# One weight load of a decode kernel, issued as four loads of unequal partition counts

## The chip, the core and the metric

The kernel runs on one core of one Trainium2 chip. A core has a matrix engine (TensorE, PE), a vector engine (VectorE, DVE), an activation engine (ScalarE, ACT), a general engine (GpSimd, POOL) and a queue processor (SyncE, SP) that here issues nearly all loads. Sixteen DMA engines carry what is issued. The metric is the device time of one execution in microseconds (us), as the median of several executions.

## The reference

One token passes through two branches whose results are added. Branch A is attention with 32 query heads over 4 cached key/value heads of 65,536 positions each, and branch B is a small mixer with an MLP behind it. Sizes: D = 1024, F = 3584, head size 128.

```python
x  = A_x;  xn = layernorm(x)
q  = xn @ wq                         # [32 heads, 128]
p  = softmax(q @ k_cache.T * 128**-0.5)          # over 65536 positions
A  = (p @ v_cache) @ wo
h  = gelu(layernorm(xn) @ w1);  hs = shift(h) @ w2
x1 = xn + hs
B  = x1 + gelu(layernorm(x1) @ w3) @ w4          # w4: 3584 x 1024
out = x + A + B
```

With one position, the four shifts of the mixer leave only zeros, so x1 is xn.

## The kernel before

Everything that the kernel reads comes through one pool of three large SBUF buffers (`big`, line 64, tiles named `slot`, 128 partitions x 64 KB). The list `slots` (lines 105 to 117) gives what each use of a buffer holds: first wq, then for each key/value head the keys and values in halves of 32,768 positions, with w3 behind the first pair and wo and w1 ahead of the last head. The very last K and V come in two loads each. The second to last use holds the last quarter of wo, w2 and piece 0 of w4; the last use holds pieces 1 to 5 of w4. The function `issue` (line 122) issues the loads of one use on SP, one `dma_start` per piece, each over all 128 partitions. `ensure` (line 145) issues a use two ahead of the one that is computed on, once its buffer is free.

w4 is laid out with 28 rows of 1024 values per partition (`w4_v`, line 76), and `W4_PIECES = (10, 7, 5, 3, 2, 1)` cuts these rows into six pieces. In this text they are w4-0 to w4-5; "the three-row piece" is w4-3, whose 128 partitions hold 3 x 2 KB = 6 KB each. `compute_w4(q)` (line 338) multiplies a piece on TensorE: two matmuls per row (`row_acc`, line 179), all added up in one PSUM tile, `psB`. After the last piece ScalarE copies `psB` out (line 346) and issues the store of the result (line 347).

The Tile framework orders instructions and adds the waits. A load signals its landing on a semaphore, and the framework gives the loads that SP and ScalarE issue eight such semaphores in turn. So a load's issue can wait for the landing of the load eight places ahead. A matmul that reads a tile waits for every load that wrote the part that it reads.

Of the kernel before, what the change touches and what calls it, by code (L numbers as in the profile page):

```python
# [18 lines left out]
HALVES = 2  # L19
LOOKAHEAD = 2  # L20
W4_PIECES = (10, 7, 5, 3, 2, 1)


@with_exitstack
def kernel(
# [14 lines left out]
    nc = tc.nc  # L40
    P = 128
# [37 lines left out]
    w2_v = B_w2.rearrange("(m c) n -> m (c n)", c=DC)  # L79
    assert sum(W4_PIECES) == FC  # L80
    w4_start = [sum(W4_PIECES[:i]) for i in range(len(W4_PIECES))]
    BIG = NT // HALVES
    BK = HALVES * KEYS

    def source(piece):
        kind = piece[0]
        if kind == "wq":
            return wq_v
        if kind == "w3":
            return w3_v  # L90
        if kind == "w1":
            return w1_v
        if kind == "w2":
            return w2_v
        if kind == "wo":
            return wo_v[piece[1]]
        if kind == "w4":
            c0 = w4_start[piece[1]]
            return w4_v[:, c0:c0 + W4_PIECES[piece[1]], :].rearrange("p c n -> p (c n)")
        _, g, t, parts = piece  # L100
        cache = A_k_cache if kind == "K" else A_v_cache
        v = cache[0, g, t * BK:(t + 1) * BK, :].rearrange("(p k) d -> p (k d)", p=P)
        return v if parts is None else v[:, parts * KEYS:(parts + 1) * KEYS]

    slots = [[("wq",)]]
    for g in range(HKV):
# [6 lines left out]
        if g == HKV - 2:  # L113
            slots.append([("wo", i) for i in range(HKV - 1)] + [("w1",)])
    n4 = len(W4_PIECES)
    slots.append([("wo", HKV - 1), ("w2",), ("w4", 0)])
# [5 lines left out]
    def issue(pieces):  # L122
        t = big.tile([P, SLOT], BF16, name="slot")
        at = 0
        for piece in pieces:
            src = source(piece)
            w = src.shape[-1]
            nc.sync.dma_start(out=t[:, at:at + w], in_=src)
            loaded[piece] = t[:, at:at + w]
            if piece[0] in ("K", "V"):  # L130
                for h in range(HALVES):
                    if piece[3] in (None, h):
                        loaded[(piece[0], piece[1], HALVES * piece[2] + h)] = t[:, h * KEYS:(h + 1) * KEYS]
            at += w
        assert at <= SLOT
# [9 lines left out]
    def ensure(upto):  # L145
        while n_issued[0] <= min(upto, len(slots) - 1):
            issue(slots[n_issued[0]])
            n_issued[0] += 1
# [71 lines left out]
    for j in range(2):  # L220
# [21 lines left out]
                          in_=sel8[:].unsqueeze(2).to_broadcast([P, 8, 16]))  # L242
# [3 lines left out]
    for b in range(2):  # L246
        for par in range(2):
            nc.vector.tensor_copy(out=psel[:, 2 * b + par, :].rearrange("p (a i) -> p a i", a=4),
                                  in_=iv[:, b, par, :].unsqueeze(1).to_broadcast([P, 4, 32]))
# [88 lines left out]
    def compute_w4(q):  # L338
        wt = loaded[("w4", q)].rearrange("p (c n) -> p c n", n=NOUT)
        for cl in range(W4_PIECES[q]):  # L340
            fc = w4_start[q] + cl
# [150 lines left out]
```

## Time and profile before

| what | value |
|---|---|
| time, median of 3 runs | 404.94 us (404.90 to 405.33) |
| the profiled execution's own time | 405.27 us |
| its span, first to last instruction | 403.5 us |
| mean granted TensorE clock | 0.831 |
| DMA | 170.10 MB, mean 422 GB/s |
| PE busy | 229.0 us, 57% of the span |
| DVE busy | 214.1 us, 53% |
| landing of the w4 pieces after issue, 2560 to 256 KB | 45.5, 25.5, 28.2, 29.6, 30.3, 27.0 us |

The page gives busy times of the engines, the span in 40 slices, and the chain of work that ended last. A line of the timeline has a start and a duration in us, the engine, the source line, the operation with its tiles (written <- read), how many there were, and in brackets how long the engine had been idle and what ended that. PEclk is the share of full speed that TensorE was granted.

### The profile page before, as it was taken

The numbers are of one execution on the slowest core, as the hardware profiler recorded it, in microseconds if no ns is written. First come the engines' busy times: TensorE is split into PE (matmuls) and PEld (weight loads), VectorE is DVE, ScalarE is ACT, GpSimd is POOL, SyncE is SP. The second block draws the span as 40 slices with busy tenths as digits, with TensorE's granted clock in tenths as the row PEclk, the third lists the DMA queues.
The fourth block names the chain that finished last, engine by engine and source line by source line (L and its number), as shares of the span: only waits on it lengthen the run. The fifth ranks groups of instructions, "written<-read, shape, count | busy, mean of one in ns | idle before, by whom it ended". The sixth has DMA issues, their size and how long they took to land.

```text
span 403.5 us, 3275 instructions
## 1 busy us (share of the span) xinstructions
PE 229.0 (57%) x1400; PEld 92.4 (23%) x1400; DVE 214.1 (53%) x244; ACT 34.7 (9%) x60; POOL 5.9 (1%) x17
## 2 busy tenths in 40 slices
PE   0038686230976295629474963586930774766754
PEld 0013232110332132204131321232410331322311
DVE  0042994001986498249737961896300984886200
ACT  0010004100021001100110020003000003002000
POOL 3000000000000000000000000000100000000000
PEclk9999698785698689659965998597795799899698
DMA  9999999999999999999999999999999999999993
GB/s 409 422 416 416 418 427 438 469 422 423 423 429 482 416 422 424 429 435 463 416 422 435 430 435 455 417 390 429 470 424 448 422 400 434 439 422 421 423 420 127
DMA packets 4900, 170.10 MB, mean 422 GB/s; under 512 B 781, under 2 KB 789, under 8 KB 1174
## 3 DMA queue, kind: packets, MB, share of 16 engines
q1 hardware_dynamic: 4608, 169.87, 97.8%
q8 instruction: 11, 0.18, 0.2%
q0 software_dynamic: 128, 0.02, 0.0%
q10 hardware_dynamic: 150, 0.01, 0.0%
q14 instruction: 3, 0.02, 0.0%
HBM read 169.88 MB, written 0.01 MB: 421 GB/s over the span
## 4 chain that ended last, share of the span: by engine, by line
DMA 61%; DVE 26%; PE 11%; ACT 1%; issue 0%; SPq 0%; DVEq 0%; ACTq 0%
DMA slot<-in_A_k_cache_dram 53%; DVE slot L359 20%; DMA slot<-in_B_w_dram 7%; PE oacc L410 4%; PE sc L363 4%; DVE mx L367 2%; PE psB L180 2%; DVE pT L400 1%; ACT p_sb L386 1%; DVE og L418 1%; PE rows L263 0%; DVE qst L276 0%; DVE m L371 0%; PE pm_mx L376 0%; PE pm_e L431 0%
## 5 line engine op out<-in xcount | busy, mean ns | idle before, releaser
L363 PE MATMUL sc<-slot,qst 128*128 128x512 bf16 x512 | 135.1, 417 | 93.3 <-DVE slot L359 93.0
L359 DVE STREAM_TRANSPOSE slot<-slot 128x2048 f32<-128x2048 f32 x64 | 143.0, 2281 | 69.7 <-DMA slot<-in_A_k_cache_dram 69.7
L363 PEld LDWEIGHTS <-qst 128*128 128x128 bf16 x512 | 51.8, 103 | 164.9 <-issue 52.4
L410 PE MATMUL oacc<-slot,pT 128*32 128x512 bf16 x512 | 45.3, 513 | 4.0 <-ACT og L415 2.1
L386 ACT ACTIVATE p_sb<-sc,nm 128x1024 bf16<-128x1024 f32 x16 | 17.8, 1114 | 175.8 <-DVE nm L383 111.8
L400 DVE STREAM_TRANSPOSE pT<-p_sb 128x1024 bf16<-128x1024 bf16 x16 | 19.9, 1244 | 16.0 <-ACT p_sb L386 16.0
L367 DVE TENSOR_REDUCE mx<-sc 128x1 f32<-128x1024 f32 x16 | 19.2, 1202 | 7.4 <-PE sc L363 7.4
L418 DVE SCALAR_TENSOR_TENSOR og<-og,alpha,oacc 128x512 f32<-128x512 f32 x12 | 9.0, 746 | 26.3 <-PE oacc L410 26.3
L410 PEld LDWEIGHTS <-pT 128*32 128x32 bf16 x512 | 16.6, 119 | 24.4 <-issue 17.0
L192 PE MATMUL pm_ln<-early 128*128 128x1 f32 x4 | 1.1, 356 | 25.8 <-DVE early L228 23.3
L369 PE MATMUL pm_mx<-ident_f,mx 128*1 128x128 f32 x16 | 4.4, 276 | 16.1 <-DVE mx L367 16.1
L180 PE MATMUL psB<-slot,dst_h 128*1 128x512 bf16 x56 | 8.0, 431 | 6.8 <-DMA slot<-in_B_w_dram 6.8
L386 ACT ACT_TABLE_LOAD x3 | 3.8, 1283 | 91.7 <-DVE nm L381 58.3
L186 DVE CAST early<-x_bf 128x8 f32<-128x8 bf16 x1 | 0.2, 172 | 21.3 <-DMA x_bf<-in_A_x_dram 21.3
L263 PE MATMUL rows<-slot,xpad 128*32 128x448 bf16 (+1 forms) x80 | 6.9, 455 | 7.5 <-DMA slot<-in_B_w_dram 7.5
L180 PE MATMUL psB<-slot,oT 128*1 128x512 bf16 x64 | 9.7, 454 | 1.1 <-DVE oT L441 1.1
L376 PE MATMUL pm_mx<-ident_f,rep 1*128 1x1 f32 x16 | 3.6, 226 | 7.4 <-DVE rep L373 7.4
L431 PE MATMUL pm_e<-og,sel8big 128*128 128x128 f32 x32 | 4.6, 288 | 5.0 <-DVE og L425 5.0
L192 PEld LDWEIGHTS pm_ln<-early 128*128 128x128 f32 x4 | 1.0, 313 | 25.8 <-issue 23.2
L376 PEld LDWEIGHTS pm_mx<-ident_f,rep 1*128 1x128 f32 x16 | 2.3, 141 | 17.8 <-DVE rep L373 17.8
L369 PEld LDWEIGHTS pm_mx<-ident_f,mx 128*1 128x1 f32 x16 | 1.3, 80 | 21.5 <-DVE mx L367 20.5
L263 PEld LDWEIGHTS <-xpad 128*32 128x32 bf16 x80 | 3.3, 118 | 10.8 <-issue 9.4
(84 smaller groups left out, 83.8 us busy)
## 6 DMA issues: line engine op xcount, KB each, us to landing
slot<-in_A_wo_dram SPq DMA_DIRECT2D x4, 2048.0 KB, 34.6
slot<-in_A_k_cache_dram SPq DMA_DIRECT2D x2, 4096.0 KB, 51.4
slot<-in_A_v_cache_dram SPq DMA_DIRECT2D x2, 4096.0 KB, 33.4
slot<-in_B_w_dram SPq DMA_DIRECT2D x1, 7168.0 KB, 42.3
slot<-in_B_w_dram SPq DMA_DIRECT2D x2, 2048.0 KB, 42.8
slot<-in_B_w_dram SPq DMA_DIRECT2D x1, 2560.0 KB, 45.5
slot<-in_B_w_dram SPq DMA_DIRECT2D x1, 1792.0 KB, 25.5
slot<-in_B_w_dram SPq DMA_DIRECT2D x1, 1280.0 KB, 28.2
```

Source lines behind the costliest of these rows:

```text
L180: nc.tensor.matmul(psB[32 * j:32 * j + 1, :], lhsT=lhsT, rhs=rhs, start=(not row_started[j]), stop=False, tile_position=(0, 32 * j), skip_ ...
L263: nc.tensor.matmul(acc[32 * j:32 * j + 32, bk, 0:width], lhsT=xp[:, c, :], rhs=wt[:, cl, ch * width:(ch + 1) * width], start=(c == 0), sto ...
L359: nc.vector.transpose(out=kf[:, cg, :], in_=kf[:, cg, :])
L363: nc.tensor.matmul(sc[:, hf, :], lhsT=qst[:, o:o + 128], rhs=kr[:, cg, hf, :, bp // 2, :, bp % 2], start=(cg == 0 and bp == 0), stop=(cg = ...
L367: nc.vector.reduce_max(out=mx[:], in_=sc[:].rearrange("p h n -> p (h n)"), axis=AX.X)
L369: nc.tensor.transpose(pm[0:1, 0:P], mx[:, 0:1], ident_f[:])
L376: nc.tensor.transpose(pm[:, P:P + 1], rep[0:1, :], ident_f[0:1, 0:1])
L386: nc.scalar.activation(out=p_sb[:], in_=sc[:], func=ACTF.Exp, bias=nm[:, 0:1], scale=SCALE, accum_out=lb[:, 0:1])
L400: nc.vector.transpose(out=pT[:], in_=p_sb[:])
L410: nc.tensor.matmul(oacc[32 * u:32 * (u + 1), :], lhsT=pT[:, hf, 32 * t:32 * (t + 1)], rhs=vt[:, :, hf, t, :], start=(hf == 0 and t < 4), s ...
L418: nc.vector.scalar_tensor_tensor(out=st["og"][:], in0=st["og"][:], scalar=alpha[:, 0:1], in1=oacc[:], op0=ALU.mult, op1=ALU.add)
L431: nc.tensor.matmul(pe[:, 0:P], lhsT=sel8big[:], rhs=og[:, 128 * cg:128 * (cg + 1)], start=(cg == 0), stop=(cg == 3), skip_group_check=True)
```

## The change

The load of w4-3 is issued as four loads in place of one. They cover partitions 0 to 24, 25 to 27, 28 to 31 and 32 to 127, and run on 5, 3, 4 and 16 DMA engines. The other loads, and all that is computed, are as before.

```diff
 W4_PIECES = (10, 7, 5, 3, 2, 1)
+
+CUTS = {("w4", 3): (25, 3, 4, 96)}
...
             src = source(piece)
             w = src.shape[-1]
-            nc.sync.dma_start(out=t[:, at:at + w], in_=src)
+            p0 = 0
+            for n in CUTS.get(piece, (P,)):
+                nc.sync.dma_start(out=t[p0:p0 + n, at:at + w], in_=src[p0:p0 + n])
+                p0 += n
+            assert p0 == P
             loaded[piece] = t[:, at:at + w]
```

## The prediction

> **What bounds the kernel now.** I read the page first: the DMA row and the rate row of its 40 slices, then the chain that ended last.
>
> ```profile
> DMA  9999999999999999999999999999999999999993
> GB/s 409 422 416 416 418 427 438 469 422 423 423 429 482 416 422 424 429 435 463 416 422 435 430 435 455 417 390 429 470 424 448 422 400 434 439 422 421 423 420 127
> DMA 61%; DVE 26%; PE 11%; ACT 1%; issue 0%; SPq 0%; DVEq 0%; ACTq 0%
> ```
>
> The DMA engines are over 90% busy in 39 of 40 slices at some 420 GB/s, so the kernel is bound by its loads. The one slice with room is the last, and the change lies there. So next the end of the chain in order of time, and the timeline of the same stretch.
>
> ```profile
> 367.66 29.56 DMA slot<-in_B_w_dram
> 397.23 0.04 issue
> 397.27 2.74 PE psB L180 x12
> 400.01 0.02 issue
> 400.03 0.58 ACT out L346
> ...
> 392.32 1.67 PE L180 MATMUL psB<-slot,dst_h 128*1 128x512 bf16 x14 [1.97 <-DMA slot<-in_B_w_dram]
> 395.42 1.24 PE L180 MATMUL psB<-slot,dst_h 128*1 128x512 bf16 x10 [1.43 <-DMA slot<-in_B_w_dram]
> 397.27 2.72 PE L180 MATMUL psB<-slot,dst_h 128*1 128x512 bf16 x12 [0.60 <-DMA slot<-in_B_w_dram]
> ```
>
> The three-row piece is the load on the chain: TensorE waits for it until 397.27, does its 6 matmuls and the 6 of the last two pieces, and ScalarE and the store follow. What a landing moves here, the end moves with it. The busy times of the last stretches show how the loads run out, and at what clock.
>
> ```profile
> core 0: us, PE busy (x) PEld busy (x) DVE busy (x) ACT busy (x) POOL busy (x), PEclk, DMA share, GB/s
> 393.70:395.30 1.60, 0.30 (x4) 0.00 (x0) 0.00 (x0) 0.00 (x0) 0.00 (x0) 1.00 1.00 407
> 395.30:397.20 1.90, 1.24 (x10) 0.43 (x10) 0.00 (x0) 0.00 (x0) 0.00 (x0) 0.98 0.56 221
> 397.20:398.60 1.40, 1.33 (x8) 0.43 (x9) 0.00 (x0) 0.00 (x0) 0.00 (x0) 0.50 0.16 61
> ```
>
> From 395.3 on DMA engines run dry one after another; 407 GB/s falls to 221 and 61. Who is late is in the trace's packet records (start, time and size of each packet). Within a load a row's packet starts as that of the row before ends, so the 16 engines' streams can be followed by linking starts to ends. The last row of the three-row piece ends at 393.39 in the first stream and at 396.77 in the last, 3.38 us later, and TensorE starts 0.5 us after that. Against the first stream, six streams lag by 0 to 0.26 us, one by 0.75, six by 1.5 to 1.9, and three by 2.8, 3.1 and 3.4. The lags are steps that stay for hundreds of us: a 16 KB instruction packet puts its stream back by about 1.5 us (one went from 0.51 to 2.03), there are 11 of them on eight streams, and the three latest streams had two each. Each stream has its own ceiling: a 64 KB row starts every 2.414 us, which is 27.1 GB/s, and a 6 KB row every 0.232 us, no faster when most others are done.
>
> **The change part by part.**
>
> 1. Rows per engine. Before: 8 rows of 6 KB on each of 16. After: 96/16 = 6 on each, plus 25/5 = 5 on five, 1 on three, 1 on four. If the small loads take the same first engines, these carry 13, 13, 13, 12 and 11 rows and eleven engines 6. The only load of one packet (x_row_bf, 2 KB) delayed a stream without 16 KB packets, so I take the first engines to be early ones and the three latest among the eleven. A late stream sheds 2 x 0.232 = 0.46 us. An early one gains at most 5 x 0.232 = 1.16 us; from a lag of 0.75 that gives 1.9, and even 1.9 + 4 x 0.232 = 2.8 stays below 3.38 - 0.46 = 2.92. If nothing else moved, the landings of this piece and of the two behind it, and the end, would come 0.46 us earlier.
>
> 2. What that sum leaves out. In a load of 128 partitions each stream goes to 8 partitions of its own, all through the kernel. Cut at 25, 28 and 32, the loads hand out other partitions, so an early stream writes the w4-3 rows for partitions that a late stream is still filling with w4-2. Is the 27.1 GB/s the stream's, or that of the way to its partitions? No row of this trace has two streams to one place. From below: crossing costs nothing, and the sum is -0.46. From above, by the one kind of row where something foreign enters a stream: 16 KB of instructions, worth 0.60 us at 27.1 GB/s, cost 1.5 us, 2.5 times its bytes. If all 8 rows of a late stream's partitions are written by others while it is busy, that would be 8 x 0.232 x 2.5 = 4.6 us, less 0.46: +4.2. I take the bytes once: 8 x 0.232 = 1.86, less 0.46, is +1.40 us. I choose it over zero because the nearest row shows that two users of one path cost at least the time of their bytes, and because the lags make the overlap certain: early streams begin the piece at 391.5, and the last is done with w4-2 at 394.90, 3.4 us or some 14 small rows later.
>
> [...]
>
> 3. Three more issues on SP. An issue took 0.33 to 0.50 us, so 1.5 us at most, on a queue that sits idle till the end. But the framework deals out eight semaphores in turn, and an issue waits for the landing eight loads earlier. Before, the last two issues wait for the two halves of the last V. After, the load of 96 waits for wo3 (last packet 376.5), the two-row piece for w2 (381.4) and the last piece for w4-0, behind which nothing else is queued on SP.
>
> ```profile
> 366.82 5.65 SPq L128 DMA_DIRECT2D slot<-in_B_w_dram  x5
> ...
> 372.14 0.33 SPq L128 DMA_DIRECT2D slot<-in_B_w_dram  x1
> ```
>
> So the last issue moves from 372.14 to about 388.0, where the wait for w4-0 ends. From the first issue (0.74) to the first packet (1.74) it took 1.0 us, so its packets can start at 389.5; the first stream that wants them does so at 394.66, or 0.46 earlier. Covered by w4-1 to w4-4 with 4.7 us to spare, I price it at nothing. Without that cover, each us that w4-0 lands beyond 392.7 would be a us of the end.
>
> 4. TensorE waits for four semaphores in place of one ahead of the w4-3 matmuls. Three have long fired; at 0.04 us of issue per step in the chain that is 0 to 0.12 us. I take 0.
>
> 5. The clock. The last 12 matmuls ran at 0.50, 0.21 us each; at full clock the row of 10 gives 0.12. If the landing moves, the half-speed window falls elsewhere. The 6 after the two-row piece bound this at 6 x 0.09 = 0.5 us in either direction. I take 0.
>
> Sum: +1.4 us. On the profiled execution (span 403.5, time 405.27) that is 406.7. This execution lies 0.33 above the median of 404.94, so the forecast is 404.94 + 1.4 = 406.3.
>
> **The rivals.**
>
> A, the other side: each engine owns its rate, crossing rows cost nothing, and the sum is part 1 alone: -0.46, 404.5; with a full clock for the last six matmuls -0.96, 404.0. For it: streams do not speed up when others run dry, as a limit inside the engine would have it. Against: a fixed place behind each stream looks the same. It decides if crossing costs under 0.46 us on the latest stream, that is two rows' time.
>
> B, nothing shifts: the latest streams are partly relieved and partly pushed back, and the crossing of two to four rows eats the gain: 404.9 + (0 to 0.46), or 404.9 to 405.4. The same time comes out if the small loads fall on engines other than I think, so that a late stream keeps 8 rows.
>
> C, the late issue of the last piece: w4-0 lands later than 392.7. Against: it lands at 387.5, ahead of every row that the change touches. 5 us of slack would have to go; 405.9 if 6 went.
>
> **How the numbers follow.** A measurement of this kernel can tell about 0.2%, 0.8 us, from no change. Crossing costs: 0.58, of which 0.52 at +0.8 or more. A: 0.27, of which 0.15 with the clock's help beyond -0.8. B: 0.13. C: 0.02. So slower 0.54 with C, faster 0.15, same the rest, 0.31. The likeliest case alone spans +0.5 (four rows, 0.93 less 0.46) to +2.7, double the cost of the six rows that a late stream moves elsewhere (1.40 + 1.39 = 2.8, rounded to the clock's doubt): 405.4 to 407.6. To hold 8 in 10 the range must take in most of A: 404.2 to 407.6. The upper bound of +4.2 needs every crossing at its worst and stays outside.
>
> **What would show it.** Rows of 6 KB that take 0.4 us or more in place of 0.24, and w4-2 rows of the late streams above 0.39, show that crossing costs; rows at 0.24 throughout, with the wait ahead of the last 12 matmuls ending near 396.8, show A. With the forecast right, that wait ends near 398.7, and the one for w4-2 later than 395.42 too. The last SP issue should stand near 388. A gap in the streams ahead of the last piece would show C. The forecast is wrong above all if 27.1 GB/s belongs to the engine and not to the way to the partitions.

## The result

The changed kernel took 408.66 us (median of 5 runs, 408.27 to 409.54) where the kernel before took 404.90 us beside it (404.76 to 405.33). The ratio is 1.010, with a 95% interval of 1.0089 to 1.0112: slower by 3.8 us. The forecast was 406.3 us, with a range of 404.2 to 407.6. Its direction came true; its size was less than half of what was measured, and the time lies outside the range.

The profiled execution has a span of 406.9 us, against 403.5. The page of the changed kernel, its DMA and rate rows over 40 slices of some 10.2 us:

```profile
DMA  9999999999999999999999999989999999999993
GB/s 406 419 413 412 434 472 400 437 426 432 477 412 414 432 445 453 412 419 438 453 438 419 414 445 451 432 377 429 474 425 445 419 406 437 425 435 412 428 326 81
```

Up to slice 38 little has moved. Slice 39 (386.6 to 396.7 us) falls to 326 GB/s where it had 420, and yet its DMA engines are as busy as before: 9 tenths or more. They carry less while they work, which is something else than running dry. The stretches of that slice in the busy-time table (columns as in the prediction; the last three are the granted clock, the DMA engines' busy share and the rate):

```profile
core 0: us, PE busy (x) PEld busy (x) DVE busy (x) ACT busy (x) POOL busy (x), PEclk, DMA share, GB/s
390.00:391.30 1.30, 1.30 (x10) 0.41 (x8) 0.00 (x0) 0.00 (x0) 0.00 (x0) 0.50 1.03 433
391.50:392.50 1.00, 1.00 (x6) 0.21 (x4) 0.00 (x0) 0.00 (x0) 0.00 (x0) 0.50 1.02 291
392.50:394.00 1.50, 1.50 (x14) 0.55 (x11) 0.00 (x0) 0.00 (x0) 0.00 (x0) 0.84 0.98 218
...
395.30:397.20 1.90, 0.00 (x0) 0.00 (x0) 0.00 (x0) 0.00 (x0) 0.00 (x0) 0.78 0.99 192
397.20:398.60 1.40, 0.37 (x2) 0.09 (x3) 0.00 (x0) 0.00 (x0) 0.00 (x0) 0.50 0.90 186
398.60:400.00 1.40, 1.40 (x10) 0.40 (x6) 0.00 (x0) 0.00 (x0) 0.00 (x0) 0.50 0.77 199
```

The same stretch of the kernel before, for one line of it:

```profile
392.50:394.00 1.50, 1.50 (x14) 0.52 (x11) 0.00 (x0) 0.00 (x0) 0.00 (x0) 1.00 0.98 397
```

At 391.5, when the first streams come to the four loads, the rate begins to fall, and from 392.5 to 400 it is about half of that 397 GB/s, at a DMA share that stays near 1 until 397. The packet records say that it is every stream: of 449 row packets after 391.0, 353 took over 1.25 times their usual duration, against 1 of 446 before. Among these slow ones, the 10 KB rows of w4-2, which the change does not touch, took 0.71 us in the median where they had taken 0.39, the 6 KB rows of w4-3 0.44 (0.235), the 4 KB rows of w4-4 0.29 (0.16). So the last packets came late: w4-2 at 397.30 (before 394.90), w4-3 at 399.97 (396.77), w4-4 at 401.53 (398.04), w4-5 at 402.18 (398.68). That is 2.4, 3.2, 3.5 and 3.5 us.

The end of the chain of waits, in order of time (start, duration, what):

```profile
367.00 31.19 DMA slot<-in_B_w_dram
398.19 0.04 issue
398.23 2.30 PE psB L186 x10
400.53 0.54 issue
401.07 2.52 PE psB L186 x11
403.59 0.02 issue
403.61 0.58 ACT out L352
```

The chain names w4-2, whose ten matmuls wait until 398.23 and run at half clock (2.30 us for 1.24), and behind them 0.54 us of "issue", time for which the view finds no releaser. That time is still a wait for w4-3. The trace records each increment of a load's semaphore, by which the load signals its landing: 16 for a load of 128 partitions, and 5, 3, 4 and 16 for the four loads of the change, which I read as the number of engines of each. The last increment of the load of 96 came at 400.98, where w4-3 had signalled at 397.23 before, and TensorE's sequencer waited on it from 398.28 to 401.01. So w4-3 bounds the end as before, and signals 3.75 us later: its last packet is 3.2 us later, and the signal came 1.01 us behind that packet where it had come 0.46 us behind. What makes that last step longer stays open.

The last 12 matmuls start at 401.07 where they had started at 397.27, 3.8 us later, and take 2.50 us where they had taken 2.72. The copy out begins at 403.61, against 400.03: 3.6 us, as far as a profiled execution goes.

### The profile page after: what moved, and what is told of

Read it like the earlier page. It is cut to its first block, busy times and chain, and to the rows that moved or that the text cites. A ratio compares the mean times of both kernels' runs of the same rounds, so it can differ in the third digit from the quotient of the medians.

```text
span 406.9 us, 3279 instructions
## 1 busy us (share of the span) xinstructions
PE 223.7 (55%) x1400; PEld 90.1 (22%) x1400; DVE 214.1 (53%) x244; ACT 34.7 (9%) x60; POOL 6.0 (1%) x17
## 4 chain that ended last, share of the span: by engine, by line
DMA 56%; DVE 25%; PE 16%; ACT 2%; issue 1%; SPq 0%; DVEq 0%; ACTq 0%
DMA slot<-in_A_k_cache_dram 43%; DVE slot L365 19%; DMA slot<-in_B_w_dram 8%; PE sc L369 5%; DMA x_bf<-in_A_x_dram 5%; PE oacc L416 4%; PE psB L186 3%; DVE mx L373 2%; PE rows L269 2%; DVE pT L406 1%; ACT p_sb L392 1%; DVE qst L282 1%; DVE og L424 1%; PE pm_mx L382 0%; DVE m L377 0%
## 5 line engine op out<-in xcount | busy, mean ns | idle before, releaser
L416 PE MATMUL oacc<-slot,pT 128*32 128x512 bf16 x512 | 37.6, 442 | 4.9 <-DVE pT L406 3.0
L416 PEld LDWEIGHTS <-pT 128*32 128x32 bf16 x512 | 14.5, 107 | 20.8 <-issue 8.5
L186 PE MATMUL psB<-slot,dst_h 128*1 128x512 bf16 x56 | 11.2, 568 | 8.7 <-DMA slot<-in_B_w_dram 8.2
L186 PE MATMUL psB<-slot,oT 128*1 128x512 bf16 x64 | 8.1, 397 | 1.1 <-DVE oT L447 1.1
L186 PEld LDWEIGHTS <-dst_h 128*1 128x1 bf16 x56 | 3.2, 107 | 16.5 <-issue 15.8
L269 PE MATMUL rows<-slot,early 128*32 128x512 bf16 x64 | 6.4, 586 | 0.0
```

The costliest lines, as they stand in the source:

```text
L186: nc.tensor.matmul(psB[32 * j:32 * j + 1, :], lhsT=lhsT, rhs=rhs, start=(not row_started[j]), stop=False, tile_position=(0, 32 * j), skip_ ...
L269: nc.tensor.matmul(acc[32 * j:32 * j + 32, bk, 0:width], lhsT=xp[:, c, :], rhs=wt[:, cl, ch * width:(ch + 1) * width], start=(c == 0), sto ...
L416: nc.tensor.matmul(oacc[32 * u:32 * (u + 1), :], lhsT=pT[:, hf, 32 * t:32 * (t + 1)], rhs=vt[:, :, hf, t, :], start=(hf == 0 and t < 4), s ...
```

## The experiments

The question after the result was why all streams ran at half their rate, and not the few that meet another in one place. Four theories stood at first. Theory 1: loads that are cut by partitions cross, that is, an engine writes to partitions that another engine fills in the 128-partition loads around it. Theory 2: loads on few engines hold the others up. Theory 3: the cut changes the order in which HBM is read. Theory 4: the issues and semaphores themselves cost the time. Each kernel of this part ran once with a profile, beside a run of the kernel before on the same chip. Single times a few tenths of a us apart prove little, since the half-clock stretch of TensorE alone falls differently from run to run (1.24 or 2.30 us for the ten matmuls of w4-2); the verdicts rest on the rates and the row packets.

The diffs show the lines that matter. Those of `CUTS` and that of "other rows of HBM" are against the changed kernel, the others against the kernel before.

### Two loads in place of four

```diff
-CUTS = {("w4", 3): (25, 3, 4, 96)}
+CUTS = {("w4", 3): (32, 96)}
```

> The three-row piece comes as two loads of 32 and 96 partitions, both on 16 engines, so every engine has 2 + 6 = 8 rows as before the change and no load runs on few engines. Theory 1, crossing (a load that hands the partitions to the engines otherwise than the 128-partition loads slows all streams): slow like the changed kernel, 407 to 409 us, rows of 6 KB at 0.4 us and more. Theory 2, loads on few engines: as before the change, 404.5 to 405.5. Theory 3, the order in which rows are read from HBM: slow, as by theory 1. Theory 4, the number of issues and the semaphore waits behind them: a third of the loss, about 406.

It took 408.52 us, beside 404.69. Both loads run on all 16 engines, 2 and 6 rows each, so no small load is left (the keys cut in 32 and 96 below give 797 packets under 512 B, and the kernel before 781: 16 more, as the changed kernel with its 5, 3 and 4 increments has 12 more), and the busy-time table shows the same fall:

```profile
392.50:394.00 1.50, 1.50 (x14) 0.52 (x9) 0.00 (x0) 0.00 (x0) 0.00 (x0) 0.70 1.05 236
```

Theory 2 falls: the whole loss is there with every load spread over 16 engines. Step 1 of the prediction, the rows per engine, is not what matters either, since here every stream has the same eight rows.

### Four loads cut by columns

```diff
-            nc.sync.dma_start(out=t[:, at:at + w], in_=src)
+            n = 4 if piece in CUTS else 1
+            for i in range(n):
+                c0, c1 = i * w // n, (i + 1) * w // n
+                nc.sync.dma_start(out=t[:, at + c0:at + c1], in_=src[:, c0:c1])
```

> The three-row piece comes as four loads again, but cut by columns: each covers 128 partitions with a quarter of the columns (1.5 KB rows). Issues, semaphores and waits are as in the changed kernel; no partition changes its engine. Theories 1 and 2: 404.5 to 405.8, a few tenths for the shorter rows. Theory 4: 408 to 409.

404.72 us, beside 404.69. The busy-time table and then the timeline of TensorE:

```profile
392.50:394.00 1.50, 1.42 (x14) 0.48 (x11) 0.00 (x0) 0.00 (x0) 0.00 (x0) 1.00 1.02 380
```

```profile
395.43 2.29 PE L185 MATMUL psB<-slot,dst_h 128*1 128x512 bf16 x16 [1.51 <-DMA slot<-in_B_w_dram]
398.59 1.03 PE L185 MATMUL psB<-slot,dst_h 128*1 128x512 bf16 x6 [0.86 <-DMA slot<-in_B_w_dram]
```

Here too are four issues, four semaphores and a last issue that waits, but each load covers all 128 partitions, as the loads around it do. The ten matmuls of w4-2 start at 395.43 (395.42 before), and the time is the same. A matmul waits here for the one or two quarters that it reads, not for all four loads as in the changed kernel; there the first of the last 12 matmuls starts 0.09 us after the last signal, against 0.04 before. Theory 4 falls, and steps 3 and 4 of the prediction, which priced the issues and the waits at nothing, hold.

### The same cut, other rows of HBM

```diff
+            if piece in CUTS:
+                src = B_w4[0:3 * P, :].rearrange("(m c) n -> m (c n)", c=3)
```

This kernel computes with other rows of w4 in place of those of w4-3; they lie one behind another in HBM.

> Cut 25, 3, 4, 96 as in the changed kernel, but the rows are read from another place of w4, where the 128 rows of 6 KB lie one behind the other in place of 56 KB apart (the piece's weights are then other ones; the work is the same). Theory 1: 408 to 409.5, as the changed kernel. Theory 3: the loss goes or changes size by half or more, 404.5 to 406.5.

408.93 us, beside 404.69:

```profile
392.50:394.00 1.50, 1.50 (x14) 0.61 (x14) 0.00 (x0) 0.00 (x0) 0.00 (x0) 1.00 1.02 228
```

The order of the reads is another, the fall the same. Theory 3 falls.

### The three small loads on top

```diff
+            if piece in CUTS:
+                p0 = 0
+                for n in CUTS[piece][:3]:
+                    nc.sync.dma_start(out=t[p0:p0 + n, SLOT - w:], in_=src[p0:p0 + n])
+                    p0 += n
             nc.sync.dma_start(out=t[:, at:at + w], in_=src)
```

w4-3 is loaded whole, and the small loads write to columns that nobody reads. In this kernel and in all those with extra loads below, the result's computation is unchanged.

> The three-row piece is one load of 128 partitions again; ahead of it the three small loads (25, 3, 4 partitions) bring the same rows a second time, to unused columns of the same buffer. Theory 1: the small loads write partitions 0 to 31 alone, which early streams own, so late streams are not touched: 404.5 to 406. Theory 2: 407 to 409.5. Theory 4: 408 to 409.

407.0 us, beside 404.69, where theory 1 had set 404.5 to 406:

```profile
392.50:394.00 1.50, 1.30 (x14) 0.52 (x14) 0.00 (x0) 0.00 (x0) 0.00 (x0) 1.00 1.02 239
```

A miss, and the telling one. The extra bytes are 192 KB, 0.46 us at 420 GB/s; the loss is 2.3 us, and for some 3 us all streams are slow, also those of other partitions: the small loads write only to 0 to 31, which by the run by step four below I read as places of eight streams. Theory 1 as I had it, where a crossing takes the time of its bytes on the stream that it meets, does not explain that. Two questions followed: is it the crossing at all, and how far does one crossing reach?

### Extra loads that cross, and extra loads that do not

Both kernels add four loads of eight rows (192 KB in all) ahead of the whole w4-3; the lines below, and those of the further extra loads, stand under a condition for that piece. All go to partitions 0 to 31, and each runs on eight streams, one row on each (its semaphore has eight increments). Which eight of the 16 these are is not shown: the records hold no engine's number.

```diff
 extra_8_consecutive
+                for i in range(4):
+                    nc.sync.dma_start(out=t[8 * i:8 * i + 8, SLOT - w:], in_=src[8 * i:8 * i + 8])
 extra_8_by_step_4
+                for i in range(4):
+                    nc.sync.dma_start(out=t[i:32:4, SLOT - w:], in_=src[i:32:4])
```

> The three-row piece is one load of 128 partitions; ahead of it four extra loads of 8 consecutive partitions (0 to 7, 8 to 15, 16 to 23, 24 to 31) bring the same rows again to unused columns. Each runs on 8 engines with one row of 6 KB. [...] Theory 1, crossing: 405.5 to 407.5, and late streams that nobody crosses slow down too, as they did with the three small loads (407.0). Theory 2, few engines: the same.

> As the run of 8 consecutive partitions, with the same number of loads, engines, rows and bytes, but each load takes every fourth partition (0, 4 .. 28, then 1, 5 .. 29 and so on), so that each of the 8 engines writes only to partitions that it has in the 128-partition loads too. Theory 1: no crossing, no loss: 404.5 to 405.2, all rows of 6 KB at 0.23 to 0.25 us. Theory 2: 405.5 to 407.5.

The consecutive ones took 406.79 us and those by step four 405.49, beside 404.81. The busy-time table of the first and of the second, and the second's TensorE in the timeline:

```profile
392.50:394.00 1.50, 1.41 (x14) 0.60 (x14) 0.00 (x0) 0.00 (x0) 0.00 (x0) 1.00 0.98 320
```

```profile
392.50:394.00 1.50, 1.50 (x14) 0.53 (x9) 0.00 (x0) 0.00 (x0) 0.00 (x0) 0.74 0.96 399
```

```profile
395.25 2.29 PE L185 MATMUL psB<-slot,dst_h 128*1 128x512 bf16 x10 [0.90 <-DMA slot<-in_B_w_dram]
```

With consecutive partitions 154 of 479 rows were slow, up to 16 at once; with a step of four, 1 of 478 (and that one shares its stream with an instruction packet). The number of streams, bytes, issues and the set of 32 partitions are the same in both, so it is the pairing of engine and partition that costs: crossing. By step four the eight streams write partitions 0 to 31 without a loss, which I read as places that they have in the 128-partition loads too. If each of the four loads hands its rows to the streams in the same order, each stream has four partitions in a row there, 0 to 3, 4 to 7, and so on to 28 to 31. By that reading, an estimate from these two runs alone, 28 of the 32 rows of the consecutive loads cross. The rate is 320 GB/s, though, not half of 397; this run is milder than the cuts.

The second kernel also shows what extra rows without a crossing cost. Its 405.49 us is 0.3 us above the range that was set for no crossing. It holds no slow row from the extra loads, but the last packet of w4-5 came at 399.31 against 398.68, and the matmuls of w4-2 fell into half clock (2.29 us).

### The extra loads to partitions 64 to 95

```diff
+                for i in range(4):
+                    nc.sync.dma_start(out=t[64 + i:96:4, SLOT - w:], in_=src[64 + i:96:4])
```

> [...] If a crossing slows only the two streams that meet (theory 1a, local), the entered streams and the intruders have rows of twice the time while both are at it, and the rest keep 0.39 us for rows of 10 KB and 0.23 for 6 KB: 405 to 406.5. If it slows all streams of the core (theory 1b, global), nearly all rows that run between 391.5 and 393 take 1.5 to 2 times as long, and the rate falls to 200 to 280 GB/s, as in the run of 8 consecutive partitions: 406 to 407.

408.28 us, beside 404.94, above both ranges; 164 of 481 rows slow, all 16 streams at once:

```profile
392.50:394.00 1.50, 1.50 (x14) 0.52 (x11) 0.00 (x0) 0.00 (x0) 0.00 (x0) 1.00 0.91 217
```

The same loads with the same step, 64 partitions further on: in place of 1 slow row there are 164, and the rate is near the half again, 217 GB/s for 397. So I read most of these rows as crossing. All streams are still slow at 395.6 to 396.5, when by the increments of the extra loads' semaphores only three engines have extra rows left. Few crossings are enough, then. How few?

### One, two and four engines in a foreign place

Two extra loads of 14 KB rows each, ahead of the whole w4-3, from rows of wq. They differ in the partitions that they write, one row for each and load. The first two kernels read the same rows of wq and differ in the partition alone.

```diff
+                for i in range(2):
+                    nc.sync.dma_start(out=t[PARTS, SLOT - 14336 + 7168 * i:SLOT - 14336 + 7168 * (i + 1)],
+                                      in_=wq_v[N * i:N * (i + 1), 0:7168])
# extra_one_own      PARTS 0:1       N 1
# extra_one_foreign  PARTS 64:65     N 1
# extra_two_foreign  PARTS 64:72:4   N 2
# extra_four_foreign PARTS 64:80:4   N 4
# extra_two_in_one   PARTS 64:66     N 2
```

> The same two loads to partition 0, which that engine has in the 128-partition loads too. Both theories: no row of another stream is longer than before, 404.5 to 405.5, as the one stream gets 28 KB (1.1 us) more and is not the last.

> In place of the 8-partition loads, two extra loads of one partition (64) with 14 KB each, on one engine. A single stream enters the partitions of one other stream for 1 to 2 us. Theory 1a: one other stream slows, the rate of all stays above 390 GB/s; 404.5 to 405.5. Theory 1b: the rate of all falls below 350 GB/s for that time; 405 to 406.5.

> Two extra loads of 14 KB rows as in the run of one foreign partition, but each of partitions 64 and 68 on two engines, so two streams each enter the partitions of another stream. One intruder slowed 8 rows of two streams and nothing else. Local rule (each crossing slows its own pair): some 16 rows of four streams at twice their time, the rate of all above 340 GB/s, 404.5 to 405.5. Coupled rule (several crossings hold up streams that none of them touches): rows of more than four streams slow at once, below 320 GB/s for a stretch.

> The same with partitions 64, 68, 72 and 76 on four engines. Local rule: eight streams slow while the two rows run, the rate at 300 to 330 GB/s for 1 to 2 us, 404.7 to 406. Coupled rule: nearly all 16 streams slow, 200 to 260 GB/s, 405 to 407.

> The same with partitions 64 and 65 on two engines: two streams enter the partitions of one. Local rule, shared in three: rows of the three streams up to three times as long (14 KB: 1.6 us; 6 KB: 0.7 us), the others as before; 404.5 to 406. Coupled rule: as with two foreign partitions, rows of streams that are not touched slow too.

The busy-time table of each, in the order of the list above:

```profile
392.50:394.00 1.50, 1.50 (x14) 0.56 (x13) 0.00 (x0) 0.00 (x0) 0.00 (x0) 0.76 0.99 400
```

```profile
392.50:394.00 1.50, 1.43 (x14) 0.49 (x11) 0.00 (x0) 0.00 (x0) 0.00 (x0) 1.00 0.93 369
```

```profile
392.50:394.00 1.50, 1.36 (x14) 0.43 (x9) 0.00 (x0) 0.00 (x0) 0.00 (x0) 1.00 1.00 233
```

```profile
392.50:394.00 1.50, 1.50 (x14) 0.59 (x11) 0.00 (x0) 0.00 (x0) 0.00 (x0) 0.74 0.97 202
```

```profile
392.50:394.00 1.50, 1.50 (x10) 0.49 (x8) 0.00 (x0) 0.00 (x0) 0.00 (x0) 0.55 1.02 310
```

One slow row in each run of this table is the one behind an instruction packet, as in the kernel before.

| extra rows | time, beside before, us | slow rows | streams slow at once |
|---|---|---|---|
| one engine to partition 0 | 404.86, 404.94 | 1 of 451 | 1 (that row's) |
| one engine to partition 64 | 404.67, 404.94 | 8 of 452 | 2, and that row's |
| two engines to 64, 68 | 405.28, 405.78 | 49 of 453 | 16 |
| four engines to 64, 68, 72, 76 | 406.68, 405.78 | 82 of 458 | 16 |
| two engines to 64, 65 | 404.99, 405.78 | 44 of 453 | 16, milder |

At partition 0 no row of the engine is slow, so that is read as its own place, and 64 as a foreign one. One engine in a foreign place is what the prediction had in mind: two streams slow each other. The second 14 KB row took 1.05 us where it takes 0.54 in its own place, the 6 KB rows of the stream that it meets 0.46 to 0.50, two rows of the intruder right behind were slow too, and nobody else is touched: 7 rows in all. As the rows read are the same as in the first kernel, theory 3 falls here too. The first 14 KB row kept its time. The rate of 369 GB/s is below the 390 that had been set for a local effect, but the rows are those of two streams only, and the time is that of the kernel before. With two engines in two foreign places all 16 streams are slow at once, and 397 GB/s becomes 233; with four it is 202. A local sharing would have left 12 of the 16 streams alone with two crossings, and 8 with four. Two engines to 64 and 65 also reach all 16, but milder: 6 KB rows at 0.72 to 0.79 in one stream and 0.30 in the others, 310 GB/s. I read that as two engines in the place of one stream.

So the step lies between one crossing and two, and numbers of crossings are not all: where several engines meet in one place (this run, and the eight consecutive partitions) 310 to 320 GB/s were left, where they enter places of their own 202 to 233. That is a reading of these runs; none tested it by itself. The times tell less than the rows here, since the extra loads are short: 14 KB rows hold a crossing for a us or two. Why the other streams are held up is not settled by these runs.

### A large load cut in two

```diff
-CUTS = {("w4", 3): (25, 3, 4, 96)}
+CUTS = {("K", 1, 0, None): (32, 96)}     # and (64, 64)
```

The first half of the keys of head 1, 8 MB, as two loads; w4-3 in one, as before.

> One load of 8 MB of keys in the middle of the kernel (first half of head 1) comes as two of 32 and 96 partitions, all else as before the change. It shows what crossing costs where all streams are in it for long. If a stream's places are shared fairly, one 64 KB row in two or three shares: 2 rows by 16 streams into 8 places take 9.6 us instead of 4.8 and the 96 part 0 to 30% more: +5 to +12 us on the 19.3 us of the load, 410 to 417. If any crossing halves the rate of all: +19 us, 424. If it costs only while two patterns overlap: +3 us, 408.

> The same load as two of 64 partitions. [...] If only the overlap of two patterns costs: +3 us, 408.

427.76 us with 32 and 96, and 429.31 with 64 and 64, beside 404.81: 23 and 24.5 us lost. The busy-time table of the kernel before, of the first and of the second:

```profile
120.00:150.00 30.00, 17.40 (x114) 7.50 (x113) 20.25 (x25) 3.04 (x7) 0.00 (x0) 0.77 0.98 424
```

```profile
120.00:150.00 30.00, 5.99 (x78) 3.18 (x76) 8.08 (x19) 2.93 (x7) 0.00 (x0) 0.71 1.00 212
```

```profile
120.00:150.00 30.00, 7.95 (x79) 3.57 (x77) 8.17 (x19) 3.25 (x7) 0.00 (x0) 0.68 1.00 206
```

The effect does not belong to the end of the kernel, nor to small rows: 64 KB rows took mostly 4.5 to 5.3 us where they take 2.42, for 46 us in the first and 48 us in the second. 8 MB take 19.8 us at 424 GB/s and 39.6 at 212, and that difference of 19.8 us is most of the 23. Of what had been expected, half the rate for all (+19 us) comes nearest.

## Why the prediction went wrong in size

**Step 1, rows per engine (-0.46 us): not seen.** No run shows a gain from fewer rows on late streams. That the small loads take the same first engines was the step's assumption, which no run shows, and that these are early ones, the three latest among the others, does not fit the runs. In the kernel with extra rows by step four, which slows no row, the last packet came 0.6 us later; and linking its streams puts lags of 0 to 0.15, 0.70, 2.19, 2.96 and 3.10 us among the eight that got extra rows. So two of its three latest streams are among those eight. In the changed kernel the load of 25 signals from four engines at 394.27 to 395.21 and from the last at 398.21, the load of 4 from three at 395.25 to 396.68 and from the last at 398.50, while all three of the load of 3 are done by 395.80. If these loads take the same first engines, as the step assumed, the fourth engine is a late one, and it was given 12 rows in place of 8, not 6: +0.93 us by the step's own price, not -0.46.

**Step 2, crossing (+1.40 us, the bytes taken once): the term that failed.** That crossing costs was right, and also the signs named for it: 6 KB rows above 0.4 us and w4-2 rows above 0.39. Its premise, that each stream has partitions of its own in the loads of 128, fits the extra rows by step four (1 slow row of 478) and those to partition 0 (1 of 451). The step netted +1.40 where w4-3 landed 3.75 us later. What was wrong is who pays. The step priced the rows of foreign partitions on the stream that they meet, a local sharing. The single foreign row behaves like that (0.54 to 1.05 us). But the change has many crossings at once, and with two places entered or more all 16 streams run at about half their rate (233 GB/s with two, 202 with four, and 186 to 222 from some 392 to 400 here, for 397). Eight us at half the rate is 4 us of loads late, and the last packets came 2.4 to 3.5 us late. The step's own upper end, +4.2, was nearer, but by luck: it priced the rows of one late stream, not a rate of all; it was worked from what an instruction packet costs a stream, and I left it outside the range because it wanted "every crossing at its worst". The rows that could have spoken for a coupling were not in the trace of before: 1 of its 446 rows after 391.0 was slow, the one behind an instruction packet. A bound should have stayed in the range for just that reason.

**Step 3, three more issues: right.** The last issue stands where it was forecast, near 388.0, in the timeline of SP:

```profile
387.89 0.35 SPq L132 DMA_DIRECT2D slot<-in_B_w_dram  x1
```

Its first 2 KB row ran at 395.7, with no gap ahead of it in its stream. The kernel cut by columns, with as many issues, took 404.72 us.

**Step 4, four semaphores: right.** The first of the last 12 matmuls starts 0.09 us after the last signal of w4-3, where it had been 0.04: +0.05 us, inside the 0 to 0.12 of the step. The 0.54 us of "issue" ahead of it are a wait for the load of 96, which signalled at 400.98, 1.01 us after the last packet of w4-3 (0.46 before).

**Step 5, the clock: right within its bound.** The last 12 matmuls gained 0.22 us. The ten of w4-2 lost 1.06 to half clock, but that cost the end nothing: they were done at 400.53, ahead of the signal at 400.98.

**The rivals.** A (crossing is free) and B (gain and loss cancel) fall with the first packet rows after 391.5. C needed w4-0 to land after 392.7; the issue that waits for it stands at 387.89.

In sum: landing of w4-3 +3.75 (3.2 by its packets, 0.55 by its later signal), the start behind it +0.05, last 12 matmuls -0.22, together +3.6 at the copy; the medians differ by 3.8.

No version here is faster than the kernel before beyond the spread of its single runs (404.69 to 405.78 us). The column cut is its equal, and every cut by partitions is slower. To give late streams fewer rows without a crossing would take a load that leaves out chosen engines, and two of the three latest (in the run by step four) are among the eight on which the loads of eight rows ran; it was not tried.

## What to carry to other kernels

When the DMA engines set the time, keep the shape of every load such that each engine writes the partitions that it writes in the loads around it: cut by columns, which cost nothing here, and not by partitions, which cost 3.8 us for 768 KB and 23 us for 8 MB. A DMA share near 1 with half the usual GB/s (0.98 and 218 GB/s for 397 here) is the sign of it, and the packets' durations tell it from streams that run dry. Where a new kind of collision is not in the trace at all, keep both bounds in the range, however unlikely the far one looks.

## What the runs showed of the hardware

Loads that sent several engines to partitions of other streams did not only slow those engines. One such engine slowed itself and the stream that it met (7 rows of 452). Two in two places slowed all 16 streams (233 GB/s for 397), and no number of crossings tried took the rate far below half over a us or more while the DMA share was 0.9 or higher: 186 to 239 GB/s with the cuts, the small loads and the extra engines in places of their own, 206 to 212 with the 8 MB load. Two engines to 64 and 65, and the loads of eight consecutive partitions, were milder (310 and 320 GB/s). A row to partition 0 under the same load kept its time (14 KB in 0.54 us), so it is neither the extra bytes nor the extra load.
